# A cross-attention block and a feed-forward layer on one core: element-wise work spread over GpSimd and ScalarE, layer-one rows in strict turn, and a new order of all pieces

## The chip, the core and the metric

The kernel runs on one core of a Trainium2 chip. The core has a matrix engine (TensorE, PE in the profile; PEld is its weight load), three element-wise engines (VectorE or DVE, ScalarE or ACT, GpSimd or POOL), and queues that start transfers (SP, ACT and POOL issue them here). Each engine runs its own instructions in their order, and semaphores hold an instruction until what it needs is there. Matmuls write PSUM; the other tiles lie in SBUF. The metric is the time of one execution in microseconds (us).

## The reference

x is 8 batches x 8 heads x 512 rows x 64, state is 8 x 8 x 32 x 64. For each batch and head:

```python
scores = scale * np.matmul(x, state.transpose(0, 1, 3, 2))
scores = scores - scores.max(-1, keepdims=True)
a = np.exp(scores)
a /= a.sum(-1, keepdims=True) + 1e-09
xread = np.matmul(a, state)
```

The same is done the other way round (the state rows attend to x): sread. Both are laid side by side, 8 x 544 rows of 512, and go through two layers:

```python
h = x @ w_in              # 4352 x 512 by 512 x 2048
r = np.maximum(h, 0.0)
g = s * (r * r) + b
return (g @ w_out).astype(np.float32)
```

## The kernel before

**The algebra.** For the rows of x the kernel never forms xread: it multiplies the state with w_in first (M, 32 states x 4 heads on 128 partitions, two groups g) and then uses A, the transposed attention weights, as the moving operand, so that h = M^T A. Layer two sums g @ w_out in PSUM; s and b enter at the end (out = s * sum + bias). For batches 5, 6 and 7 and for the state rows layer two is a 2 x 2 block product with 7 instead of 8 products, for which sums of blocks of g (S) and of w_out (wsum, T1 to T4) are formed.

**Pieces and order.** All work is cut into pieces, and the constant ORDER (L15 to L75, nine strings) lists them. The loop at L713 takes them in that order, and each engine gets its instructions in that order; nothing is moved afterwards. An engine letter at the end (A ScalarE, V VectorE, G GpSimd) says who does a piece. For a batch b: x and xn load x in two layouts (GpSimd's queue; x waits, through a tiny GpSimd copy, for the transpose of the batch before, L180); xT transposes (VectorE); T are the score matmuls; U transposes the scores back (VectorE, from PSUM); mu takes the maxima and D subtracts them (L320); E1 is the exponential (ScalarE); z sums and inverts; At scales (L336) and A transposes (VectorE). keep copies the scores (ScalarE); nm, nms, E2, a2, aps, a2T, V, srd make sread. M.b.j.own are the matmuls of a quarter of M, own choosing one of two PSUM pairs, and Mc its copy to SBUF. l.b.f is one block of 128 layer-one rows for 512 tokens: two matmuls of 512 columns into one of two PSUM banks, then a relu on ScalarE (L449). lh is the same for half the tokens and two blocks (batch 0). s.b.f.n.e squares n blocks (L464), sh a half. L.b.rr.q is a quarter of a layer-two product for 128 tokens (4 matmuls), out its eviction and store. P, ev and put are products, evictions and stores of the 7-product form, 8 matmuls of 256 columns to a P; lsr, ssr, S_sr, P_sr, ev_sr are the same for the state rows. win and wout load the weights, turn and pair prepare the state, cps, c and bias make the bias, castx and casts convert what was loaded as float32, idle.n issues n matmuls whose result nobody reads.

**Tiles that bind pieces together.** Relu outputs lie in tiles of four blocks, three of them in a pool (L455, halves in four, L481). A tile comes free when all its squares are done. Two PSUM banks take layer-one results, two layer-two results, and two pairs of banks (own or not) everything else.

## Time and profile before

| | |
|---|---|
| median of 3 runs | 225.02 us (224.21 to 225.16) |
| the profiled execution | 224.36 us, of which the instructions span 222.2 us |
| TensorE busy | 210.7 us, 95% of the span |
| VectorE busy | 183.6 us, 83%, 267 instructions |
| ScalarE busy | 141.8 us, 64% |
| GpSimd busy | 43.4 us, 20%, mostly issue of transfers |
| granted TensorE clock | 1.0 |

Busy time says how long an engine had an instruction in work. An instruction that stands still after it started, because something it shares is taken, counts as busy. In the profile's rows `out<-in` names what is written and read, then the shape per operand, the number of instructions, the busy time and the mean duration in ns; what follows the second bar is the idle time of the engine before them and what ended it. In a timeline row the first number is the start in us from the span's start, the second the duration. Matmul rows overlap: one of 512 columns is shown 379 ns long while the next starts after 216.

### The profile page before, as it was taken

To read this page: it belongs to the slowest core of one execution; us is meant where nothing else is said; L and a number is where in the kernel's file an instruction comes from. 1 tells how busy PE (TensorE), PEld (TensorE's weight loads), DVE (VectorE), ACT (ScalarE), POOL (GpSimd) and SP (SyncE) were. 2 spreads that over 40 slices of the span, in tenths; PEclk is the share of its full clock that TensorE was granted. 3 is DMA by queue.
4 is the path that set the end of the run, shared out by engine and by line. 5 is a ranking of instruction groups with operands and counts; after the bars stand their busy time and mean duration, and the time that the engine had idled before them with its cause. 6 is when DMAs were issued, how large, how long until landed. Compare 5 with 4: busy or idle time off the path is not lost.

```text
span 222.2 us, 4473 instructions
## 1 busy us (share of the span) xinstructions
PE 210.7 (95%) x1816; PEld 115.8 (52%) x1816; DVE 183.6 (83%) x267; ACT 141.8 (64%) x243; POOL 43.4 (20%) x73
## 2 busy tenths in 40 slices
PE   6469999999999999999999999999999999999992
...
DVE  1597998889769997989796799889999997966772
...
POOL 8245504000273400046002160005200000000000
...
GB/s 158 227 207 206 205 193 58 101 72 20 100 112 117 112 174 50 16 100 120 192 47 133 96 128 124 49 45 101 141 2 65 127 0 3 94 99 0 3 134 149
DMA packets 23416, 22.67 MB, mean 102 GB/s; under 512 B 4196, under 2 KB 16996, under 8 KB 23396
## 3 DMA queue, kind: packets, MB, share of 16 engines
...
## 4 chain that ended last, share of the span: by engine, by line
PE 88%; DMA 4%; DVE 3%; ACT 3%; SPq 1%; issue 0%
PE ops L496 31%; PE hps L452 24%; PE opf_X L137 9%; PE opf_W L137 5%; PE mps L137 4%; DMA xf<-in_x_dram 4%; PE hps_sr L452 3%; PE opf_Y L137 2%; PE vps L137 2%; PE T_None L137 2%; PE aps L137 2%; PE ops_sr_X L137 2%; ACT M L152 1%; DVE xT L289 1%; PE ops_sr_W L137 1%; ACT rh L482 1%
## 5 line engine op out<-in xcount | busy, mean ns | idle before, releaser
L456 ACT ACTIVATE r<-hps 128x512 f16<-128x512 f32 x120 | 69.3, 610 | 29.8 <-PE hps L452 28.4
L496 PE MATMUL ops<-w_out,g 128*128 128x512 f16 x320 | 78.1, 379 | 1.3 <-DVE g L462 1.3
L452 PE MATMUL hps<-A,M 128*128 128x512 f16 x240 | 65.3, 380 | 0.5 <-DVE M L152 0.3
L496 PEld LDWEIGHTS <-g 128*128 128x128 f16 x320 | 30.3, 98 | 38.4 <-issue 2.8
L462 DVE TENSOR_TENSOR g<-r 128x1024 f16<-128x1024 f16 (+1 forms) x39 | 34.5, 897 | 8.1 <-ACT r L456 8.0
L452 PEld LDWEIGHTS <-M 128*128 128x128 f16 x240 | 21.9, 98 | 25.8 <-issue 4.7
L137 PEld LDWEIGHTS <-g 128*128 128x128 f16 x288 | 28.0, 98 | 6.4 <-issue 0.2
L152 ACT CAST M<-mps 128x1024 f16<-128x1024 f32 x28 | 28.0, 1013 | 1.8 <-PE mps L137 1.8
L192 POOL DMA_DIRECT2D xn<-in_x_dram x32 | 18.5, 588 | 29.2 <-PE vps L137 28.3
L506 DVE SCALAR_TENSOR_TENSOR osb<-ops,sb_bc,bias_bc 128x512 f32<-128x512 f32 x20 | 14.7, 734 | 1.0 <-PE ops L496 1.0
L180 POOL COPY ahead<-xT 1x2 f16<-1x2 f16 x5 | 1.8, 367 | 67.0 <-DVE xT L289 67.0
L456 ACT ACTIVATE r_sr<-hps_sr 128x256 f16<-128x256 f32 x16 | 6.2, 385 | 12.8 <-PE hps_sr L452 12.4
L564 DVE TENSOR_TENSOR g<-g 128x1024 f16<-128x1024 f16 x18 | 12.2, 685 | 2.0 <-PE opf_Y L137 1.9
L289 DVE STREAM_TRANSPOSE xT<-xh 128x1024 f32<-128x1024 f32 (+2 forms) x12 | 10.3, 871 | 3.2 <-ACT xh L152 3.2
L333 DVE TENSOR_REDUCE z<-E 128x32 f32<-128x1024 f16 (+1 forms) x9 | 9.9, 1095 | 3.7 <-ACT E L328 3.7
L137 PE MATMUL opf_X<-w_T,g 128*128 128x256 f16 x96 | 11.9, 273 | 0.0
L137 PE MATMUL mps<-w_in,stT 64*32 64x512 f16 x256 | 11.2, 383 | 0.2 <-ACT M L152 0.2
L318 DVE TENSOR_REDUCE mu<-U 128x32 f32<-128x1024 f32 (+1 forms) x9 | 9.9, 1097 | 0.2
L376 ACT ACTIVATE E<-T_None,nms 128x512 f16<-128x512 f32 x8 | 5.5, 691 | 6.9 <-DVE nms L372 4.4
L328 ACT ACTIVATE E<-Dm 128x1024 f16<-128x1024 f32 (+1 forms) x9 | 8.7, 963 | 1.8 <-DVE Dm L322 1.5
L322 DVE TENSOR_TENSOR Dm<-U,mu 128x1024 f32<-128x1024 f32 (+1 forms) x8 | 9.6, 1201 | 0.2
L314 DVE STREAM_TRANSPOSE U<-T_None 128x1024 f32<-128x1024 f32 x7 | 8.7, 1247 | 1.2 <-PE T_None L137 0.8
...
## 6 DMA issues: line engine op xcount, KB each, us to landing
...
w_in<-in_moe_w_in_dram POOLq DMA_DIRECT2D x8, 256.0 KB, 10.6
...
```

What stands on the lines that cost most here:

```text
L137: return nc.tensor.matmul(out, lhsT, rhs, start=start, stop=stop, tile_position=tp, is_transpose=is_transpose, skip_group_check=skip,)
L152: (engine.copy if engine is nc.scalar else engine.tensor_copy)(out, in_)
L192: nc.gpsimd.dma_start(out=xn_t[b][32 * jh : 32 * jh + 32].rearrange("t h c d -> t h (c d)"), in_=x[b].rearrange("h (t jh c) d -> jh t h (c ...
L289: nc.vector.transpose(part(out, p, g), part(in_, p, g))
L318: nc.vector.tensor_reduce(part(mu, p), blk(part(at[b]["U"], p)), AX.X, ALU.max)
L333: nc.vector.tensor_reduce(part(z, p), blk(part(at[b]["E1"], p)), AX.X, ALU.add)
L452: nc.tensor.matmul(hps, lhsT, rhs, start=(i == 0), stop=(i == len(terms) - 1))
L456: nc.scalar.activation(R_t[tag, q][:, i], hps, AF.Relu)
L462: e.tensor_mul(g, r, r)
L496: nc.tensor.matmul(ops_t[tag, rr], G_t[tag][:, f, P * rr : P * rr + P], w_out_f(f), start=(f == 0), stop=(f == NKF - 1),)
L506: nc.vector.scalar_tensor_tensor(osb, ops_t.pop((tag, rr)), s_bc, bias_bc, ALU.mult, ALU.add)
L564: e.tensor_tensor(out, x, y, op)
```

## The change

It edits three things. (1) ORDER is rewritten whole: the same pieces but for their engines, PSUM pairs and grouping. To GpSimd go the subtractions of maxima of batches 2, 4, 5 and 6 (that of batch 3 was there before), the At of batch 2, three more half squares of batch 0, ten squares of two blocks and one of four, block sums of batches 5 to 7 and of the state rows, and two weight sums. To ScalarE go squares of two blocks, seven of the eight squares of the state rows, and some evictions of M, while VectorE takes others and most a2T copies. In the first string the loads of x for batch 1 and of the later weights stand further back, partly behind squares on GpSimd. (2) The three relu tiles, and the four of half size, become single-buffer pools used in strict turn (`in_turn`). (3) The sums of blocks take a third choice, 2, for both halves in one instruction (`HALVES`).

```diff
-    "win.0 win.1 wout.0 x.1 win.2 wout.1 win.3 wout.2 wout.3 idle.11 castx.1.0.V castx.0.0.A xT.0.0.0 "
-    "casts.A turn.0.4.A pair.0.4 xT.0.1.0 T.0.1.0 U.0.0 mu.0.0 sb castx.1.1.A castx.0.1.A D.0.V.0 "
-    "xT.0.0.1 idle.6 xT.0.1.1 E1.0.0 T.0.0.1 keep.0.0 M.0.0.1 Mc.0.0.A z.0.0 At.0.V.0 A.0.0 idle.4 "
-    "M.0.1.1 Mc.0.1.A lh.0.0.0 U.0.1 mu.0.1 D.0.V.1 lh.0.2.0 keep.0.1 sh.0.0.0.V sh.0.2.0.V E1.0.1 z.0.1 "
-    "At.0.V.1 L.0.1.0 lh.0.6.0 sh.0.6.0.G L.0.0.0 M.1.0.1 Mc.1.0.A lh.0.4.0 A.0.1 lh.0.6.1 xT.1.0 "
-    "sh.0.4.0.G xT.1.1 T.1.1 U.1 lh.0.0.1 lh.0.4.1 lh.0.2.1 sh.0.2.1.G mu.1 M.0.2.0 Mc.0.2.A L.0.0.1 x.2 "
-    "L.0.1.1 st D.1.V sh.0.6.1.V keep.1 l.0.9 l.0.8 M.0.3.1 Mc.0.3.V l.0.10 s.0.8.2.V cps.0 cps.1 E1.1 "
-    "l.0.13 z.1 l.0.11 s.0.10.2.V At.1.V M.1.1.1 l.0.12 Mc.1.1.A l.0.14 l.0.15 L.0.0.2 s.0.12.2.A M.1.2.1 "
-    "A.1 s.0.14.2.V Mc.1.2.A cps.2 cps.3 c L.0.1.2 l.1.1",
...
+    "win.0 castx.0.0.V castx.1.0.A xT.0.1.0 casts.A xT.0.0.0 idle.12 pair.0.4 T.0.1.0 castx.1.1.A "
+    "turn.0.4.A M.0.0.0 U.0.0 mu.0.0 D.0.V.0 E1.0.0 idle.3 z.0.0 castx.0.1.V xT.0.0.1 keep.0.0 xT.0.1.1 "
+    "Mc.0.0.A T.0.0.1 keep.0.1 win.1 wout.0 M.0.1.1 At.0.V.0 A.0.0 Mc.0.1.A win.2 lh.0.2.0 x.1 U.0.1 "
+    "lh.0.0.0 sh.0.0.0.G sb mu.0.1 D.0.V.1 lh.0.6.0 idle.3 E1.0.1 z.0.1 At.0.V.1 A.0.1 lh.0.4.0 xT.1.0 "
+    "M.1.0.1 sh.0.2.0.G L.0.1.0 M.0.2.0 Mc.1.0.A M.1.2.1 Mc.1.2.V wout.1 L.0.0.0 Mc.0.2.A lh.0.6.1 "
+    "lh.0.4.1 cps.0 l.0.8 sh.0.4.0.G lh.0.2.1 xT.1.1 T.1.1 keep.1 sh.0.6.0.G l.0.10 l.0.9 L.0.0.1 "
+    "lh.0.0.1 U.1 mu.1 cps.1 l.0.11 win.3 sh.0.2.1.G M.0.3.1 Mc.0.3.A D.1.V E1.1 L.0.1.1 M.1.1.1 l.0.13 "
+    "l.0.15 wout.2 s.0.10.2.V s.0.8.2.V L.0.1.2 Mc.1.1.A l.0.14 z.1 l.0.12 s.0.12.2.A At.1.V A.1 L.0.0.2 "
+    "wout.3 s.0.14.2.A cps.2 cps.3 M.1.3.1 c",
+    "l.1.0 l.1.3 bias st pair.4.16 L.0.0.3 l.1.2 x.2 xT.2 Mc.1.3.A out.0.0 L.0.1.3 x.3 l.1.6 l.1.9 T.2.1 "
+    "keep.2 out.0.1 sh.0.0.1.V l.1.10 turn.4.12.A l.1.1 L.0.3.0 l.1.5 M.2.1.0 Mc.2.1.A sh.0.4.1.G "
+    "sh.0.6.1.G M.2.0.1 Mc.2.0.A U.2 mu.2 D.2.G L.0.2.0 L.0.3.1 s.1.0.4.V l.1.12 l.1.4 xT.3 T.3.1 E1.2 "
+    "M.2.2.0 l.1.14 x.4 l.1.13 L.0.3.2 l.1.7 l.1.11 U.3 L.0.2.1 z.2 At.2.G l.1.8 nm.3 nms.3.A E2.3.1 "
+    "E2.3.0 Mc.2.2.V A.2 s.1.4.4.V L.0.3.3 l.1.15 L.0.2.2 L.0.2.3 l.2.3 M.3.2.1 M.2.3.0 Mc.2.3.A l.2.6 "
+    "l.2.7 out.0.3 L.1.0.0 turn.12.16.A s.1.8.2.V s.1.10.2.V out.0.2 s.1.12.4.V l.2.2 l.2.10 mu.3 L.1.0.1 "
+    "Mc.3.2.A l.2.11 xn.3 L.1.1.0 a2.3 aps.3 xT.4 s.2.2.2.V l.2.1 L.1.1.1 l.2.5 x.5 a2T.3.V l.2.8 M.3.0.1 "
+    "Mc.3.0.A M.3.1.0 Mc.3.1.V",
...
+    "l.3.0 aps.4 out.1.2 l.3.8 l.3.11 T.5.1 a2T.4.V V.4 nm.5 nms.5.A E2.5.1 l.3.12 L.2.1.0 s.2.14.2.G U.5 "
+    "L.2.0.2 mu.5 l.3.5 E2.5.0 nm.2 z.4 s.2.12.2.G L.2.1.1 nms.2.A L.2.0.3 out.2.0 l.3.13 l.3.10 srd.4 "
+    "s.3.0.4.G L.2.1.2 l.3.6 At.4.V D.5.G l.3.15 L.2.1.3 out.2.1 M.5.1.1 l.3.9 s.3.8.2.V l.3.14 L.3.1.0 "
+    "l.3.7 L.2.2.0 s.3.6.2.A A.4 s.3.4.2.A L.2.2.1 M.4.3.1 M.5.0.0 L.2.2.2 Mc.5.0.A x.6 L.2.2.3 Mc.5.1.V "
...
+    "l.4.2 L.2.3.0 out.3.1 l.4.4 U.6 mu.6 D.6.G L.3.2.0 nm.6 l.4.6 L.2.3.1 L.2.3.2 A.5 L.2.3.3 out.2.3 "
+    "E1.6 z.6 L.3.2.1 s.4.0.2.G nms.6.A L.3.2.2 l.4.12 l.4.14 L.3.2.3 l.4.10 At.6.V l.4.15 L.3.0.0 "
+    "s.4.12.4.A L.3.0.1 E2.6.1 l.4.7 a2.2 E2.6.0 aps.2 out.3.2",
...
+    "l.5.13 l.5.8 a2.0 aps.0 a2T.0.A L.4.1.2 l.5.5 l.5.10 L.4.1.3 xn.0 l.5.14 wsum.T2.1.G l.5.6 L.4.0.2 "
+    "l.5.4 M.6.3.1 nm.7 Mc.6.3.A V.6.0 L.4.0.3 srd.0 srd.6 l.5.7 s.5.6.2.G U.7 wsum.T2.0.V s.5.4.2.A "
+    "M.7.2.0 out.4.1 xn.7 wsum.T4.0.V wsum.T4.1.V M.7.0.1 L.4.2.0 mu.7 A.6 l.6.11 l.6.9 nms.7.A L.4.2.1 "
+    "s.5.12.4.V s.5.8.4.V out.4.0 l.6.3 Mc.7.0.V P.5.0 l.6.15 l.6.1 E2.7.0 Mc.7.2.A L.4.2.2 L.4.2.3 nm.1 "
+    "D.7.V l.6.8 S.5.3.0.V S.5.1.0.V E1.7 P.5.1 l.6.13 E2.7.1 out.4.2 P.5.2 ev.5.X1 M.7.1.0 S.5.3.1.G "
+    "M.7.3.1 Mc.7.3.A l.6.12 S.5.2.0.V P.5.4 S.5.1.1.V S.5.2.1.V l.6.10 P.5.3 a2.7 ev.5.Y z.7",
+    "l.6.0 P.5.5 l.6.14 P.5.6 P.5.7 Mc.7.1.A l.6.6 aps.7 l.6.4 ev.5.X2 P.5.8 P.5.9 S.5.4.2.G ev.5.W1 "
+    "l.6.5 l.6.7 P.5.10 s.6.8.2.V s.6.10.2.V At.7.V A.7 s.6.12.4.V ev.5.X3 s.6.0.2.A nms.1.A l.6.2 "
+    "s.6.2.2.A a2T.7.V E2.1.0 P.5.11 E2.1.1 ev.5.W2 l.7.7 s.6.4.2.V s.6.6.2.V P.5.12 P.5.13 ev.5.X4 "
+    "S.6.3.0.V put.5.0.0 S.6.3.1.V l.7.3 P.6.0 P.6.1 l.7.1 S.6.1.2.V l.7.10 xn.1 V.7 srd.7 l.7.2 a2.1 "
+    "put.5.0.1 P.6.2 l.7.6 P.6.3",
+    "l.7.0 S.6.2.2.V ev.6.X1 P.6.4 l.7.8 aps.1 l.7.4 l.7.5 s.7.4.4.A ev.6.Y P.6.5 a2T.1.A ev.6.X2 l.7.15 "
+    "P.6.6 l.7.9 P.6.8 P.6.9 P.6.7 ev.6.W1 ev.6.X3 V.1 srd.1 l.7.13 S.6.4.2.G P.6.10 s.7.0.2.G s.7.2.2.G "
+    "l.7.12 lsr.3 P.6.11 l.7.14 put.5.1.0 put.5.1.1 l.7.11 S.7.3.0.V P.6.12 S.7.1.0.V ev.6.W2 put.6.0.0 "
+    "P.6.13 s.7.10.2.A lsr.11 s.7.8.2.V s.7.12.4.V P.7.0 lsr.2 lsr.7 ev.6.X4 P.7.1 S.7.3.1.V P.7.2 lsr.6 "
+    "lsr.5 ssr.2.2.A P.7.3 lsr.9 S.7.1.1.G S.7.2.2.V ev.7.X1 lsr.1 P.7.4",
+    "lsr.0 lsr.10 ssr.0.2.A P.7.6 lsr.8 ssr.8.2.A lsr.13 P.7.5 ssr.6.2.A ev.7.Y lsr.12 ssr.12.2.A ev.7.X2 "
+    "lsr.15 P.7.7 S.7.4.2.G ssr.10.2.A lsr.4 lsr.14 P.7.8 ssr.14.2.A P.7.9 ssr.4.2.V ev.7.W1 P_sr.0 "
+    "put.6.0.1 ev.7.X3 P.7.10 P.7.11 S_sr.3.0.G S_sr.1.2.G P.7.12 P.7.13 put.6.1.0 put.6.1.1 ev.7.W2 "
+    "ev_sr.0.0.X.0.0 P_sr.1 S_sr.2.2.V put.7.0.0 ev.7.X4 S_sr.4.0.G P_sr.2 ev_sr.0.1.X.0.0 put.7.0.1 "
+    "S_sr.3.1.G ev_sr.0.0.Y.1.1 put.7.1.0 put.7.1.1 S_sr.4.1.G P_sr.3 ev_sr.1.1.W.0.0 P_sr.4 P_sr.5 "
+    "ev_sr.1.1.X.1.1 ev_sr.0.1.W.1.1 P_sr.6 ev_sr.1.0.X.0.1",
@@ -446,13 +445,19 @@
             G_t[tag] = whole_t[tag][:, :, :ntok]
         return G_t[tag]
 
+    turns = {}
+
+    def in_turn(shape, name, tag, n):
+        k = turns[tag] = turns.get(tag, -1) + 1
+        return rpool.tile(shape, FP16, name=name, tag=f"{tag}{k % n}", bufs=1)
+
     def layer1(tag, f, terms, ntok):
         hps = ps_h.tile([P, ntok], FP32, name=f"hps_{tag}_{f}", tag="ph")
         for i, (lhsT, rhs) in enumerate(terms):
             nc.tensor.matmul(hps, lhsT, rhs, start=(i == 0), stop=(i == len(terms) - 1))
         q, i = f // 4, f % 4
         if (tag, q) not in R_t:
-            R_t[tag, q] = rpool.tile([P, 4, ntok], FP16, name=f"r_{tag}_{q}", tag="r")
+            R_t[tag, q] = in_turn([P, 4, ntok], f"r_{tag}_{q}", "r", 3)
         nc.scalar.activation(R_t[tag, q][:, i], hps, AF.Relu)
 
     def squared(e, g, r):
@@ -478,7 +483,7 @@
             for g in range(NG):
                 lhsT = M[:, g, P * (f + i) : P * (f + i) + P]
                 mm(hps[:, i, :], lhsT, part(A, p, g)[:, 0, :], start=(g == 0), stop=(g == NG - 1))
-        r = R_t[b, f, p] = rpool.tile([P, 2, HALF], FP16, name=f"rh_{b}_{f}_{p}", tag="rh", bufs=4)
+        r = R_t[b, f, p] = in_turn([P, 2, HALF], f"rh_{b}_{f}_{p}", "rh", 4)
         nc.scalar.activation(r, hps, AF.Relu)
 
     def square_half(b, f, p, e):
@@ -517,15 +522,16 @@
             store(b, rr, [rows.rearrange("(t r j) n -> r j t n", r=SCH, j=4)[rr]])
 
 
+    HALVES = (slice(0, 4), slice(4, 8), slice(0, 8))
     fast_w = {}
 
     def weight_sum(name, h, e):
 
         if name not in fast_w:
             fast_w[name] = konst.tile([P, NKF // 2, HALF], FP16, name=f"w_{name}", tag=f"w_{name}")
-        w = w_out16[:, 8 * h : 8 * h + 8]
-        B = [[w[:, k::2, HALF * n : HALF * n + HALF] for n in range(2)] for k in range(2)]
-        T = {k: t[:, 4 * h : 4 * h + 4] for k, t in fast_w.items()}
+        w = w_out16
+        B = [[w[:, k::2, HALF * n : HALF * n + HALF][:, HALVES[h]] for n in range(2)] for k in range(2)]
+        T = {k: t[:, HALVES[h]] for k, t in fast_w.items()}
         a, b = {
             "T1": lambda: (B[0][1], B[0][0]),
             "T2": lambda: (B[1][1], T["T1"]),
@@ -554,11 +560,12 @@
 
     def act_sum(b, name, h, e):
 
-        A = lambda i, j: block(b, i, j)[:, 4 * h : 4 * h + 4]
+        sl = HALVES[h]
+        A = lambda i, j: block(b, i, j)[:, sl]
         out, x, y, op = {
             1: lambda: (A(1, 0), A(1, 0), A(1, 1), ALU.add),
             2: lambda: (A(0, 0), A(1, 0), A(0, 0), ALU.subtract),
-            3: lambda: (fast(b, "S3")[:, 4 * h : 4 * h + 4], A(0, 0), A(1, 0), ALU.subtract),
+            3: lambda: (fast(b, "S3")[:, sl], A(0, 0), A(1, 0), ALU.subtract),
             4: lambda: (A(0, 1), A(0, 1), A(0, 0), ALU.subtract),
         }[name]()
         e.tensor_tensor(out, x, y, op)
@@ -618,7 +625,7 @@
             "S3": (A(0, 0), A(1, 0), ALU.subtract),
             "S4": (A(0, 1), S_sr("S2"), ALU.subtract),
         }[name]
-        out, x, y = (t[:, 4 * h : 4 * h + 4] for t in (S_sr(name), x, y))
+        out, x, y = (t[:, HALVES[h]] for t in (S_sr(name), x, y))
         e.tensor_tensor(out, x, y, op)
 
     def w_block(j, n):
```

## The prediction

> **What bounds the kernel now.** I read the page first (engine shares, slices, the chain that ended last), then the waits of TensorE, then the timeline of the start, then the pairs of VectorE and GpSimd instructions that ran at the same time, and last the groups by shape for prices.
>
> ```profile
> PE 210.7 (95%) x1816; PEld 115.8 (52%) x1816; DVE 183.6 (83%) x267; ACT 141.8 (64%) x243; POOL 43.4 (20%) x73
> ...
> PE   6469999999999999999999999999999999999992
> ...
> DVE  1597998889769997989796799889999997966772
> ...
> POOL 8245504000273400046002160005200000000000
> ...
> PE 88%; DMA 4%; DVE 3%; ACT 3%; SPq 1%; issue 0%
> ```
>
> TensorE is full from the fourth slice to the end. The second view, TensorE's waits between 31 and 218 us, has one entry:
>
> ```profile
> PE hps L452 <- ACT r L456: 0.2, 1, 0.2
> ```
>
> In the timeline matmuls of 512 columns start every 0.216 us there and those of 256 every 0.109, with 0.093 more at each change of tile shape; after 30.5 us no other gap is over 0.04 us. So only two things can shorten this kernel: the first 30 us, and the 4.1 us from the last matmul (218.1) to the end (222.2). Anything else can only lengthen it. The start:
>
> ```profile
> 10.36 0.62 ACT L152 CAST xh<-xf 128x512 f16<-128x512 f32 x1 [1.38 <-DMA xf<-in_x_dram]
> 10.89 0.62 ACT L328 ACTIVATE E<-Dm 128x512 f16<-128x512 f32 x1
> ...
> 12.66 1.01 ACT L152 CAST M<-mps 128x1024 f16<-128x1024 f32 x1 [0.68 <-PE mps L137]
> ...
> 13.40 0.71 DVE L358 STREAM_TRANSPOSE A<-At 128x512 f16<-128x512 f16 x1
> ...
> 16.07 0.75 DVE L462 TENSOR_TENSOR g<-rh 128x512 f16<-128x512 f16 x2
> ...
> 16.55 1.04 PE L496 MATMUL ops<-w_out,g 128*128 128x512 f16 x4 [1.35 <-DVE g L462]
> ```
>
> ScalarE's second cast of x waits for its transfer and holds the first exponential 1.3 us; the first A is ready at 14.1, layer one starts at 14.2, and the first layer two waits for squares. From 14.2 to 30.5 the matmul starts leave 3.4 us unused (1.5, 0.1, 0.2, 0.4, 0.4, 0.4, 0.4).
>
> The view for what the change adds, pairs of VectorE and GpSimd at one time:
>
> ```profile
> 24.16 1.04 POOL L462 TENSOR_TENSOR g<-rh 128x512 f16<-128x512 f16 x1 [2.24 <-ACT rh L482]
> 24.17 2.11 DVE L322 TENSOR_TENSOR Dm<-U,mu 128x1024 f32<-128x1024 f32 x1
> ...
> 37.12 1.06 POOL L462 TENSOR_TENSOR g<-rh 128x512 f16<-128x512 f16 x1
> 37.18 0.75 DVE L506 SCALAR_TENSOR_TENSOR osb<-ops,sb_bc,bias_bc 128x512 f32<-128x512 f32 x1
> ...
> 70.36 1.27 DVE L343 TENSOR_TENSOR At<-E,rz 128x1024 f16<-128x1024 f16 x1
> 70.50 1.14 POOL L180 COPY ahead<-xT 1x2 f16<-1x2 f16 x1 [4.02 <-DVE xT L289]
> ```
>
> A VectorE subtraction (median 1.22) took 2.11 beside a GpSimd square of 1.04: it stood still until that was over. A GpSimd copy of 0.17 took 1.14 behind a VectorE product. So two-operand work in SBUF on the two engines excludes each other. An eviction out of PSUM kept its 0.73 to 0.75, and a transpose beside the square at 18.74 its 0.71.
>
> **The change, part by part.** Prices:
>
> ```profile
> L462 DVE TENSOR_TENSOR g<-r 128x2048 f16<-128x2048 f16 x16 | 19.4, 1214 | 2.2 <-ACT r L456 2.1
> L460 ACT ACTIVATE g<-r 128x2048 f16<-128x2048 f16 x2 | 3.8, 1910 | 0.1
> L462 POOL TENSOR_TENSOR g<-rh 128x512 f16<-128x512 f16 x4 | 4.2, 1060 | 4.5 <-ACT rh L482 4.4
> L322 POOL TENSOR_TENSOR Dm<-U,mu 128x1024 f32<-128x1024 f32 x1 | 1.9, 1907 | 4.5 <-DVE mu L318 4.5
> ```
>
> Moved to GpSimd: 1024 f16 elements I take at 2 x 1.06 = 2.1 us and 2048 at 4.2 (lower ends 1.9 and 3.8, by the 1907 row). With 7 half squares (7.4 us), 5 subtractions (9.5), 10 squares of two (21), one of four (4.2), block sums of batches 5 to 7 (2 x 2.1 + 3 x 4.2 = 16.8), state-row sums (4 x 1.06 + 2.1 = 6.3), two weight sums (4.2) and one At (2.1), GpSimd computes 71.6 us instead of 6.1. The At has no row: 2.1 by size, or 4.0, since on VectorE its permuted write costs 1.29 against 0.68 for a square; I take 2.1; the other end is counted at l.2.6 below.
>
> All other engines, counted over both orders with these rows: VectorE 195.8 to 168.3 (the page's 183.6 is 0.94 of the sum, because neighbours overlap), ScalarE 157.7 to 166.3, TensorE the same 340 pieces with 73 changes of tile shape in each and 18 dummy matmuls for 21 (at the start, beside waits). So relief of VectorE is worth nothing by itself: TensorE did not wait for it after 31 us.
>
> The swaps of M evictions, a2T copies and nms between ScalarE and VectorE (1.01 against 1.21, 1.02 against 0.67, 0.20 against 0.17) and of M's PSUM banks lie beside matmuls: nothing. The last seven state-row products keep their order; before them GpSimd's chain (S_sr.3, S_sr.1, S_sr.4: 1.06 + 2.1, 0.7 on VectorE, 3 x 1.06 = 7.0 us) starts 8.7 us of matmuls ahead of its last reader, so the 4.1 us tail stays. The squares of batch 7 and S.6.4 on GpSimd (4.2 + 2 x 2.1) end 1.1 us before the relu of lsr.3, which takes their tile: nothing while the prices hold.
>
> The start, walked through the new order: win.0 still lands at 10.6. VectorE now casts x for g=0 (transfer at 5.2), so T begins at 6.9 (6.63 before). The exponential follows its subtraction at 9.9, not 10.9; but VectorE then does castx.0.1, two transposes (1.35 us) before At, and A.0.0 is ready at 14.4 (14.1 before). The first squares run on GpSimd: 16.5 to 18.6, so L.0.1.0 starts at 18.6 instead of 16.55, with four layer-one halves and M.1.0 ahead of it. x.1 is issued behind win.2 and lands at 20.4 instead of 17.8. wout.1, win.3, wout.2, wout.3 are queued behind GpSimd squares, that is behind relus: wout.3 is issued at 26 (16.8 before) and lands at 32.7, just ahead of cps.3. L.0.0.3 then waits 0.3 us for s.0.14 on ScalarE and ends at 36.15; before it ended at 36.03 with the bias product (0.22) still to come, so 36.25 for the same work: -0.1. (By unused TensorE time it is 2.7 us for 3.4, layer one 0.3 later: -0.4. I take the end, which holds everything.)
>
> After it, the exclusion and the strict turn together. The turn makes the relu that opens a new four-row tile wait for the squares of the tile three earlier. In the old order these squares always stand ahead of that relu; in the new one they stand behind it seven times (l.2.6, l.3.8, l.3.12, l.4.10, l.6.11, l.6.6, lsr.11), so the relu, and all of ScalarE behind it, waits for VectorE or GpSimd. I counted TensorE's slots along the order (0.216, 0.109, 0.093 for a change of shape, 10.9 us for the start) and looked at each place where a GpSimd operation meets a VectorE one or such a relu. Four are tight, times from the span's start:
> - T.3.1, due 44.4. D.2.G and s.1.0.4.V become ready within 0.5 us (41.1 to 41.7). If the square wins, xT.3 behind it ends at 44.2: 0. If the subtraction wins, the square waits 1.9 and T.3.1 starts at 46.1: 1.8. I take half, 0.9.
> - l.2.6, due 53.3: VectorE's A.2 waits for At.2.G (47.8 to 49.9), then s.1.4, out.0.3, s.1.8, s.1.10 end at 53.8: 0.2; with the At at 4.0 us 2.1, with the square first above 0. I take 0.2.
> - P.5.0, due 150.2, reads s.5.6.2.G, ready at 147.2 and 2.1 long. VectorE's s.5.12.4.V and s.5.8.4.V (1.21 each) come at 147.1 to 149.5. Between them GpSimd ends at 150.4 (0.2, but then s.5.8 holds relu l.6.3 and l.6.1: 0.8), behind both at 151.7 (1.5), ahead 0. I take 0.8.
> - l.6.5, due 166.1, needs the relu of l.6.6, which waits for s.6.10.2.V, which follows s.6.8.2.V behind S.5.4.2.G (4.2 us from 159.7 or, behind the scaling of a2.7, 160.5): the relu ends at 165.9 or 166.7: 0 to 1.0 with GpSimd a little late. I take 0.6.
>
> Waiting costs VectorE elsewhere too, but there it stays under TensorE: in the string from l.1.0 24.7 us of work plus 1.7 of expected waits (GpSimd's share times the expected rest of an operation, times nine instructions) against 27.4, from l.7.0 11.5 + 4.9 against 22.1.
>
> The last item hangs on whether the scaling of a2 (L385, one tensor operand) excludes GpSimd; no row shows the two together, so its ends are 0.1 and 0.6. [...]
>
> Sum: -0.1 + 0.9 + 0.2 + 0.8 + 0.6 = +2.4 us; ends -0.1 and +6.3. The profiled execution took 224.36 us (span 222.2) and would take 226.8; the median shown, 225.02, is 0.66 above it, so the forecast is 227.4.
>
> **The rivals.**
>
> Hidden anyway, 225.0: the four places come out at their lower ends and TensorE stays gapless. For it: from 155 to 172 us VectorE was busy 16.6 of 17.0 us and left no gap; its load now falls by 27 us. Against: 71.6 us of GpSimd work whose prices rest on five instructions.
>
> Faster, 223.4: the start closes half of the 3.4 us (1.6). For it: the exponential a microsecond earlier, M.0.0 at 10.8 instead of 12.2, three layer-one pieces of batch 0 ahead of L.0.0.1. Against: A.0.0, x.1 and the first L later. It decides if layer one starts by 14.2, unused time by 36 us is under 2 us and the waits after it are under 0.5.
>
> Slower through the clock, 227: dummy matmuls stand at 1.5 to 5.6 and 11.1 to 11.8, and between T (7.6) and M.0.0 (10.7) TensorE does almost nothing for 3.1 us; before, the longest hole was 2.3 us (9.0 to 11.5) and spacing stayed 0.216. The first six dummies started every 0.427. If that spacing comes back at 11 us, the 2.7 us of matmuls to 18.6 take double, of which 0.7 falls into waits: +2. [...] No row here shows a hole that long.
>
> The change not doing what it says: the strict turn may be the turn that tiles took before; the seven relus wait all the same, since three tiles are all there are.
>
> **How the numbers follow.** Exclusion and turn 0.42 (227.4), clock 0.08 (227), hidden 0.25 (225.0), start 0.25 (223.4). About 0.5%, 1.1 us, is what a measurement here tells from no change. Slower 0.50, within it 0.25, faster 0.25. The range goes down to the start's case and up to 230.0, where the two largest upper ends (1.8, 2.1) and the 0.8 and 0.6 meet (225.0 - 0.1 + 5.3 = 230.2); the slower case's own range is 226.2 to 230.0.
>
> **What would show it.** Gaps of TensorE at T.3.1, l.2.6, P.5.0 and l.6.5, and a VectorE square of 2 to 3 us beside D on GpSimd; ScalarE's relus of l.2.6 and l.6.6 released by VectorE squares; GpSimd rows of 2.1 and 4.2; first A at 14.4, first L at 18.6, x.1 at 20.4. Wrong if TensorE's waits after 36 us sum under 0.5 us; if GpSimd's rows are 1.3 times longer (then lsr.3's relu is 1.4 us late, and the time passes the range); or if x.1 or wout land 3 us later than walked.

## The result

| | before | after |
|---|---|---|
| median (lowest to highest, 4 runs each) | 225.09 us (224.21 to 225.94) | 231.12 us (230.32 to 231.65) |
| ratio, 95% interval | | 1.0265 (1.0215 to 1.0316) |
| the profiled execution, and its span | 224.36 us, 222.2 us | 230.93 us, 229.2 us |
| last matmul starts | 217.86 us | 223.65 us |
| from there to the end | 4.36 us | 5.51 us |

The changed kernel is slower by 6.0 us (its profiled execution by 6.6, between the spans 7.0). The forecast was 227.4 with a range up to 230.0, so the direction held and the size did not. The medians leave out an execution over 1.5% above the fastest of its kernel, such as the profiled one of e3 below (233.90 us at a granted clock of 0.968). From the page of the changed kernel, the engine shares, the slices of TensorE and of its clock, and the chain that ended last:

```profile
PE 214.3 (93%) x1813; PEld 116.6 (51%) x1813; DVE 172.1 (75%) x219; ACT 149.5 (65%) x257; POOL 108.4 (47%) x104
...
PE   7697989699999999999999999999799999999990
...
PEclk9859999999999999999999999999999999999999
...
PE 71%; DVE 13%; DMA 4%; ACT 4%; POOL 3%; issue 3%; DVEq 0%; ACTq 0%
```

GpSimd went from 20% to 47%, VectorE from 83% to 75%. But VectorE's share of the chain rose from 3% to 13%: it does less, and TensorE waits for it more. TensorE's row has a 6 in slice 8 (41 us) and a 7 in slice 29 (160 us), where it had nines from the fourth slice on, and PEclk drops to 5 in the third slice.

The waits of TensorE between 36 and 225 us (total, times, longest):

```profile
PE ops L501 <- DVE g L467: 1.9, 1, 1.9
PE opf_Y L136 <- DVE osb L511: 1.2, 1, 1.2
PE hps L457 <- DVE M L151: 0.4, 1, 0.4
```

Before, this view had one entry of 0.2. By start-to-start times, with the usual spacing and the 0.09 us of a change of tile shape taken off, the gaps of TensorE after 36 us sum to 4.5 us: 2.04 at L.0.3.0 (41.4 us), 1.36 at P.5.2 (160.3; the expectations below call this place P.5.3), 0.53 at a layer-one block that waits for the eviction Mc.5.3 (134.9), and 0.58 in six gaps of 0.04 to 0.29. The work that ended at 36.25 us before ends at 37.63, so 1.4 us was lost ahead of it. With the 1.15 us by which the tail grew, that makes the 7.0 us between the two spans. The two large gaps, the tail and the start follow.

**At 41 us.** The timeline of VectorE, GpSimd and TensorE, start and duration first:

```profile
38.63 1.25 DVE L288 STREAM_TRANSPOSE xT<-xh 128x1024 f32<-128x1024 f32 x1 [0.48 <-DMA xh<-in_x_dram]
...
39.80 1.36 DVE L511 SCALAR_TENSOR_TENSOR osb<-ops,sb_bc,bias_bc 128x512 f32<-128x512 f32 x2
...
39.94 0.17 POOL L179 COPY ahead<-xT 1x2 f16<-1x2 f16 x1 [9.74 <-DVE xT L288]
40.17 1.07 POOL L182 DMA_DIRECT2D xh<-in_x_dram  x2
...
41.08 2.51 DVE L467 TENSOR_TENSOR g<-rh 128x512 f16<-128x512 f16 x1
...
41.24 2.06 POOL L467 TENSOR_TENSOR g<-rh 128x512 f16<-128x512 f16 x2
...
43.65 0.61 PE L501 MATMUL ops<-w_out,g 128*128 128x512 f16 x2 [1.88 <-DVE g L467]
```

VectorE's half square sh.0.0.1 takes 2.51 us where that shape took 0.415 before. It starts 0.16 us ahead of two half squares that GpSimd does back to back, sh.0.4.1 and sh.0.6.1, while GpSimd is still issuing the load of x.3 (the row at 40.17), and it ends after both. L.0.3.0 reads its result.

**At 160 us.** The same view for the product P.5.2, whose bank out.4.2 has to empty:

```profile
154.38 2.32 POOL L191 DMA_DIRECT2D xn<-in_x_dram  x4
...
156.15 1.78 DVE L321 TENSOR_TENSOR Dm<-U,mu 128x1024 f32<-128x1024 f32 x1
156.72 3.19 POOL L571 TENSOR_TENSOR S<-g 128x1024 f16<-128x1024 f16 x1
157.85 2.60 DVE L571 TENSOR_TENSOR S<-g 128x1024 f16<-128x1024 f16 x1
160.49 0.69 DVE L571 TENSOR_TENSOR g<-g 128x1024 f16<-128x1024 f16 x1
161.10 0.74 DVE L511 SCALAR_TENSOR_TENSOR osb<-ops,sb_bc,bias_bc 128x512 f32<-128x512 f32 x1
```

D.7 (1.22 alone) starts while GpSimd is issuing four loads, and ends 1.22 us after the last of them. GpSimd's S.5.3.1, ready at 156.72, stands until D.7 is over, and S.5.3.0 on VectorE (the row at 157.85, 0.69 alone; the expectation of e3 calls it S.5.1.0) stands until S.5.3.1 is over. So the eviction out.4.2 (the last row) comes 1.2 us too late.

**The tail.** SyncE's queue and VectorE's last eviction:

```profile
221.37 0.55 SPq L706 DMA_DIRECT2D out_dram<-osr  x1
221.96 2.52 SPq L608 DMA_DIRECT2D out_dram<-osx  x4
...
223.96 0.48 DVE L702 SCALAR_TENSOR_TENSOR osr<-ops_sr_X,sb_bc,bias_bc 128x256 f32<-128x256 f32 x1 [0.39 <-PE ops_sr_X L136]
224.58 1.85 SPq L706 DMA_DIRECT2D out_dram<-osr  x3
```

Four stores of batch 7 (put.7) stand ahead of the last three stores of the state rows. Before, the four state-row stores were the last thing in the queue (217.00 to 219.51 us).

**The start.** Two places in the timeline of the first 33 us:

```profile
18.88 2.04 POOL L467 TENSOR_TENSOR g<-rh 128x512 f16<-128x512 f16 x2
19.02 2.47 DVE L344 TENSOR_TENSOR At<-E,rz 128x512 f16<-128x512 f16 x1
...
22.28 0.92 PE L136 MATMUL hph<-A,M 128*128 128x256 f16 x7 [1.27 <-DVE A L357]
...
25.53 1.04 POOL L467 TENSOR_TENSOR g<-rh 128x512 f16<-128x512 f16 x1 [3.38 <-ACT rh L487]
26.52 1.56 POOL L205 DMA_DIRECT2D w_out<-in_moe_w_out_dram  x2
28.06 1.04 POOL L225 DMA_DIRECT2D stn<-in_state_dram  x1
29.07 1.12 POOL L182 DMA_DIRECT2D xh<-in_x_dram  x2
...
32.12 1.02 PE L501 MATMUL ops<-w_out,g 128*128 128x512 f16 x4 [0.70 <-DMA w_out<-in_moe_w_out_dram]
```

At.0.V.1 takes 2.47 us (0.69 before) beside two more back-to-back squares. And GpSimd's queue holds the loads wout.2, wout.3, st and x.2 behind sh.0.2.1, which waited 3.4 us for its relu: x.2 is issued at 29.1 us and lands at 38.6 (before: 25.1 and 33.5).

Prices, from the groups by shape of the changed kernel, GpSimd first, then VectorE; the second number after the bar is the mean of one in ns:

```profile
L467 POOL TENSOR_TENSOR g<-r 128x1024 f16<-128x1024 f16 x10 | 19.0, 1917 | 20.4 <-ACT r L461 19.9 <-PE ops L501 0.5
L571 POOL TENSOR_TENSOR g<-g 128x2048 f16<-128x2048 f16 x3 | 12.2, 4064 | 20.4 <-PE opf_Y L136 20.4
```

```profile
L384 DVE TENSOR_SCALAR a<-E,q 128x512 f16<-128x512 f16 x16 | 10.9, 720 | 0.3
```

The scaling of a2 on VectorE, 350 ns each before, takes 720.

### The profile page after: what moved, and what is told of

It reads as the page before. It is cut to its first block, busy times and chain, and to the rows that moved or that the text cites. A ratio compares the mean times of both kernels' runs of the same rounds, so it can differ in the third digit from the quotient of the medians.

```text
span 229.2 us, 4475 instructions
## 1 busy us (share of the span) xinstructions
PE 214.3 (93%) x1813; PEld 116.6 (51%) x1813; DVE 172.1 (75%) x219; ACT 149.5 (65%) x257; POOL 108.4 (47%) x104
## 4 chain that ended last, share of the span: by engine, by line
PE 71%; DVE 13%; DMA 4%; ACT 4%; POOL 3%; issue 3%; DVEq 0%; ACTq 0%
PE ops L501 21%; PE hps L457 17%; PE opf_X L136 8%; PE opf_W L136 5%; DMA xh<-in_x_dram 4%; PE hps_sr L457 3%; PE mps L136 3%; PE opf_Y L136 2%; PE dps L667 2%; POOL g L467 2%; PE vps L136 2%; PE hph L136 2%; DVE g L467 2%; ACT r L461 2%; PE ops_sr_X L136 2%
## 5 line engine op out<-in xcount | busy, mean ns | idle before, releaser
L457 PE MATMUL hps<-A,M 128*128 128x512 f16 x240 | 66.5, 380 | 0.5 <-DVE M L151 0.4
L467 POOL TENSOR_TENSOR g<-r 128x1024 f16<-128x1024 f16 (+1 forms) x11 | 22.6, 2070 | 21.8 <-ACT r L461 21.2
L571 POOL TENSOR_TENSOR g<-g 128x2048 f16<-128x2048 f16 (+1 forms) x4 | 14.3, 3577 | 28.7 <-PE opf_Y L136 20.4
L151 ACT CAST M<-mps 128x1024 f16<-128x1024 f32 x23 | 22.9, 1012 | 1.5 <-PE mps L136 1.5
L467 DVE TENSOR_TENSOR g<-r 128x1024 f16<-128x1024 f16 (+1 forms) x23 | 20.4, 909 | 1.7 <-ACT r L461 1.7
L191 POOL DMA_DIRECT2D xn<-in_x_dram x32 | 18.6, 591 | 4.8 <-PE vps L136 3.8
L321 POOL TENSOR_TENSOR Dm<-U,mu 128x1024 f32<-128x1024 f32 x5 | 10.4, 2085 | 20.1 <-DVE mu L317 20.1
L465 ACT ACTIVATE g<-r 128x1024 f16<-128x1024 f16 (+1 forms) x13 | 15.1, 1185 | 0.2
L511 DVE SCALAR_TENSOR_TENSOR osb<-ops,sb_bc,bias_bc 128x512 f32<-128x512 f32 x20 | 14.4, 728 | 1.1 <-PE ops L501 1.1
L600 DVE SCALAR_TENSOR_TENSOR osx<-opf_X,sb_bc,bias_bc 128x512 f32<-128x512 f32 x9 | 6.6, 737 | 7.9 <-PE opf_X L136 7.7
L151 DVE CAST M<-mps 128x1024 f16<-128x1024 f32 x9 | 10.8, 1207 | 1.9 <-PE mps L136 1.9
L467 POOL TENSOR_TENSOR g<-rh 128x512 f16<-128x512 f16 x7 | 7.2, 1046 | 10.5 <-ACT sb_bc L640 7.1
```

The costliest lines, as they stand in the source:

```text
L151: (engine.copy if engine is nc.scalar else engine.tensor_copy)(out, in_)
L191: nc.gpsimd.dma_start(out=xn_t[b][32 * jh : 32 * jh + 32].rearrange("t h c d -> t h (c d)"), in_=x[b].rearrange("h (t jh c) d -> jh t h (c ...
L321: e.tensor_tensor(blk(part(Dm, p)), blk(part(at[b]["U"], p)), over_n(part(at[b]["mu"], p)), ALU.subtract)
L457: nc.tensor.matmul(hps, lhsT, rhs, start=(i == 0), stop=(i == len(terms) - 1))
L465: nc.scalar.activation(g, r, AF.Square)
L467: e.tensor_mul(g, r, r)
```

## The experiments

The theory after the result: VectorE and GpSimd shut each other out, and where the new order sets their operations side by side TensorE sees it; the tail is a matter of SyncE's queue. The rivals: the new order or the strict turn costs the time whoever does the work; the loads in GpSimd's queue are late; the lower clock at the start.

| run | edit to the changed kernel | median us | ratio to before, 95% |
|---|---|---|---|
| e1 | 29 operations back to VectorE | 248.47 | 1.1024 (1.0942 to 1.1106) |
| e2 | two half squares to VectorE | 231.50 | 1.0293 (1.0201 to 1.0385) |
| e3 | S.5.3.1 to VectorE | 229.34 | 1.0202 (1.0137 to 1.0267) |
| e4 | last stores issued by ScalarE | 230.17 | 1.0251 (1.0176 to 1.0325) |
| e5 | four loads ahead of one square | 230.04 | 1.0235 (1.0179 to 1.0291) |
| e6 | e3 + e4 + e5 | 227.68 | 1.0142 (1.0093 to 1.0191) |
| e7 | no strict turn | 231.71 | 1.0310 (1.0244 to 1.0376) |
| e8 | kernel before, four D on GpSimd | 224.67 | 1.0004 (0.9974 to 1.0034) |
| e9 | e6 + e2 + win.3 ahead of a square | 226.68 | 1.0088 (1.0057 to 1.0119) |
| e10 | e9 + six dummy matmuls | 226.91 | 1.0111 (1.0063 to 1.0158) |
| e11 | e9 + xT.2 behind c | 226.51 | 1.0067 (1.0044 to 1.0090) |
| e12 | e11 + s.3.0.4 to VectorE, Mc.5.3 earlier | 233.28 | 1.0362 (1.0328 to 1.0395) |
| e13 | all loads ahead of all squares | 229.16 | 1.0183 (1.0130 to 1.0236) |
| e14 | e13 + the mends, s.3.0.4 left on GpSimd | 225.00 | 1.0017 (0.9989 to 1.0045) |

### e1: the work back on VectorE

```diff
- ... sh.0.0.0.G ... D.2.G ... At.2.G ... s.3.0.4.G ... S.5.3.1.G ... S_sr.4.1.G ...
+ ... sh.0.0.0.V ... D.2.V ... At.2.V ... s.3.0.4.V ... S.5.3.1.V ... S_sr.4.1.V ...
```

> The changed kernel, but 29 of the 31 operations that the change newly gave to GpSimd are done by VectorE at the same place of the order (two squares, s.2.12.2 and s.5.6.2, stay on GpSimd). Order, strict turn and tail are unchanged. Theory (VectorE and GpSimd shut each other out): VectorE's scaling of a2 falls back from 720 ns to about 350, the gap of 2.0 us at L.0.3.0 and that of 1.4 us at P.5.3 shrink to under 0.3 each, and the time is about 228 us; the later start (1.1) and the longer tail (1.2) stay. Rival (the new order and the strict turn cost the time, whoever does the work): the two gaps stay and the time is 230 to 232 us. Second rival (GpSimd really relieved VectorE): VectorE is late now and the time is over 232 us.

It took 248.47 us, 17 more than the changed kernel, so the second rival came closest, in a way nobody had: VectorE was busy 182 us (74% of the span), so it is not full, but it does its work in order, and the places in the order were written for GpSimd. The first and a later gap of TensorE, 4.3 and 4.6 us, are such places. At 18.4 us L.0.1.0 needs sh.0.2.0, which now stands on VectorE behind a reduction that waits for an exponential, behind At, A and xT.1.0. The timeline of e1:

```profile
19.12 0.69 DVE L332 TENSOR_REDUCE z<-E 128x16 f32<-128x512 f16 x1 [0.70 <-ACT E L327]
...
21.91 0.67 DVE L288 STREAM_TRANSPOSE xT<-xh 128x512 f32<-128x512 f32 x1
...
22.50 0.38 DVE L467 TENSOR_TENSOR g<-rh 128x512 f16<-128x512 f16 x1
22.94 1.03 PE L501 MATMUL ops<-w_out,g 128*128 128x512 f16 x2 [4.18 <-DVE g L467]
```

Of the two gaps that the run was made for, the one at P.5.2 was gone, and at L.0.3.0 1.06 us was left, where the theory had under 0.3 for each. The part of the theory on the scaling is clean here. The scaling of a2 in the groups of e1, with GpSimd nearly out of the way:

```profile
L384 DVE TENSOR_SCALAR a<-E,q 128x512 f16<-128x512 f16 x16 | 5.1, 361 | 0.3
```

720 ns beside GpSimd's work, 361 without, 350 before: an instruction with one tensor operand is held too. The mutual hold is real, and giving the work back is no cure, because this order was written for two queues.

### e2: the two half squares at 41 us

```diff
- ... sh.0.4.1.G sh.0.6.1.G M.2.0.1 ...
+ ... sh.0.4.1.V sh.0.6.1.V M.2.0.1 ...
```

> The changed kernel, but the two half squares sh.0.4.1 and sh.0.6.1 go from GpSimd to VectorE. Theory: sh.0.0.1 on VectorE stood 2.1 us behind them; it takes 0.41 us now, the gap at L.0.3.0 falls from 2.0 to about 0.1 us, the squares cost VectorE 0.8 us that TensorE does not see, and the time is about 229.2 us. Rival (the load of x for batch 2 is late, the transpose with it and all that VectorE has behind it): the gap stays above 1 us and the time within 0.5 us of 231.

Measured 231.50, no gain. The three half squares took 1.09 us on VectorE and the gap at L.0.3.0 was gone, as the theory said. In its place came 1.0 us at T.2.1 and 1.6 us at T.3.1, where VectorE's transposes waited for x. From the timeline of e2:

```profile
48.46 1.25 DVE L288 STREAM_TRANSPOSE xT<-xh 128x1024 f32<-128x1024 f32 x1 [0.93 <-DMA xh<-in_x_dram]
```

x.3 landed at 48.3. It is issued only when xT.2 is done, and xT.2 waited for x.2. So there are two causes at this place, and the gap that is seen is the larger of them. Not all of it is the edit's: this execution was already 0.9 us behind the changed kernel's at 33 us, ahead of the edit, and x.2 landed at 40.4 and not at 38.6. The wait at T.3.1 comes back in e9 (1.56). At T.2.1 and T.3.1 the gaps given for the experiments hold the 0.09 us of the change of shape.

### e3: the block sum at 160 us

```diff
- ... M.7.1.0 S.5.3.1.G M.7.3.1 ...
+ ... M.7.1.0 S.5.3.1.V M.7.3.1 ...
```

> The changed kernel, but the block sum S.5.3.1 goes from GpSimd to VectorE. Theory: D.7 and S.5.1.0 on VectorE no longer wait beside it (1.8 and 2.6 us fall to 1.2 and 0.7), the eviction out.4.2 comes in time and the gap of 1.36 us ahead of P.5.3 goes: about 229.8 us. Rival (VectorE is simply full there, since it held 16.6 of 17 us before): the 0.7 us more on VectorE keep the gap at 0.7 us or more and the time above 230.5.

229.34 us, 1.8 under the changed kernel (229.10 to 229.90, against 230.32 to 231.65); the gap of 1.36 was gone. The timeline of this place is shown from e6 below, which holds this edit:

```profile
155.39 1.22 DVE L321 TENSOR_TENSOR Dm<-U,mu 128x1024 f32<-128x1024 f32 x1
156.52 0.68 DVE L571 TENSOR_TENSOR S<-g 128x1024 f16<-128x1024 f16 x1
...
158.24 0.75 DVE L511 SCALAR_TENSOR_TENSOR osb<-ops,sb_bc,bias_bc 128x512 f32<-128x512 f32 x1 [0.31 <-PE ops L501]
```

The subtraction is back at 1.22 and the block sum at 0.68, and now VectorE waits for TensorE. VectorE had room for the work; it had no room to be held.

### e4: the queue of the last stores

```diff
-            nc.sync.dma_start(out_sr[i][:, :, sl], out[:, sl])
+            nc.scalar.dma_start(out_sr[i][:, :, sl], out[:, sl])
```

> The changed kernel, but the last four stores of the state rows are issued by ScalarE, not behind the stores of batch 7 in SyncE's queue. Theory (the tail grew because the last stores stand behind four stores of batch 7 in that queue): the time from the last matmul's start to the end falls from 5.45 to about 4.2 us, and the time is about 229.9 us. Rival (the transfers themselves are slower, because more of them run at the end): the tail stays above 5 us and the time at 231.

In the profile the tail fell from 5.51 to 4.07 us, which is 0.3 us shorter than in the kernel before. The median is 230.17, 0.95 under the changed kernel's, with intervals that overlap; the tail itself is the measure. The queues of SyncE and ScalarE in the timeline of e4:

```profile
217.54 5.22 SPq L608 DMA_DIRECT2D out_dram<-osx  x8
...
221.16 3.65 ACTq L706 DMA_DIRECT2D out_dram<-osr  x4
```

The last store is issued at 224.26 us, right behind its eviction (223.75); before the edit that was 225.87 for 223.96.

### e5: four loads ahead of a square

```diff
- ... win.3 sh.0.2.1.G ... wout.2 s.0.10.2.V ... wout.3 s.0.14.2.A ... bias st pair.4.16 ... x.2 xT.2 ...
+ ... win.3 wout.2 wout.3 st x.2 sh.0.2.1.G ... s.0.10.2.V ... s.0.14.2.A ... bias pair.4.16 ... xT.2 ...
```

> The changed kernel, but in GpSimd's queue the loads wout.2, wout.3, st and x.2 stand ahead of the half square sh.0.2.1 (behind win.3) instead of behind it; every computation is where it was, those on GpSimd too. Theory (the square, which waits for a relu until 25.5 us, holds the loads behind it in GpSimd's queue; x.2 is issued at 29.1 us instead of about 25 and lands at 38.6, so the transpose xT.2, the evictions and sh.0.0.1 on VectorE and the two half squares on GpSimd, which stand behind the load of x.3, all come late and meet): x.2 is issued by 25.5 us, the wait for wout.2 (0.9 with the change of shape) and the gap of 2.0 us at L.0.3.0 are gone, together 2.5 to 3 us, and the time is about 228.4 us. Rival (the exclusion alone makes the gap): the gap at L.0.3.0 stays above 1.5 us and the time above 230.

x.2 was issued at 24.81 instead of 29.07, as expected, and the gap with the wait for wout.2 fell from 0.87 to 0.20. But x.2 landed only 0.9 us earlier (37.73), 12.9 us after its issue where the changed kernel had 9.5; win.3, wout.2, wout.3 and st were issued in the 3.8 us ahead of it, which is probably the reason; no run was made for that. The gap at L.0.3.0 stayed at 1.75, and the median was 230.04. The rival on the exclusion was right about that gap. The timeline of e5 says why it cannot be moved by a load:

```profile
37.76 1.25 DVE L288 STREAM_TRANSPOSE xT<-xh 128x1024 f32<-128x1024 f32 x1
38.93 1.37 DVE L511 SCALAR_TENSOR_TENSOR osb<-ops,sb_bc,bias_bc 128x512 f32<-128x512 f32 x2
39.07 0.17 POOL L179 COPY ahead<-xT 1x2 f16<-1x2 f16 x1 [12.05 <-DVE xT L288]
39.30 1.14 POOL L182 DMA_DIRECT2D xh<-in_x_dram  x2
40.21 2.58 DVE L467 TENSOR_TENSOR g<-rh 128x512 f16<-128x512 f16 x1
40.44 2.06 POOL L467 TENSOR_TENSOR g<-rh 128x512 f16<-128x512 f16 x2
```

Both queues hang on xT.2. VectorE does two evictions after it and comes to sh.0.0.1 2.45 us after xT.2 began; GpSimd waits for xT.2, issues x.3 and comes to its squares 2.68 us after xT.2 began. In the changed kernel these were 2.45 and 2.61, in the run with all loads in front 2.41 and 2.66. The order itself makes them meet, whenever x.2 lands.

### e6: three mends at once

The edits of e3, e4 and e5 together.

> The loads moved as in the run with the loads first, S.5.3.1 on VectorE, and the last four stores issued by ScalarE. If the three causes stand beside each other: 231.1 - 2.7 - 1.4 - 1.3 = 225.7 us. If one mend only moves the wait to the next place (as the two half squares on VectorE did): 227.5 us or more.

227.68 us: above the 225.7 of "beside each other" and within the rival's bound. The tail (4.07) and P.5.2 (no gap) came in full; 1.55 us stayed at L.0.3.0 and 2.16 us ahead of the layer-one half that waits for A.0.1.

### e7: without the strict turn

```diff
-            R_t[tag, q] = in_turn([P, 4, ntok], f"r_{tag}_{q}", "r", 3)
+            R_t[tag, q] = rpool.tile([P, 4, ntok], FP16, name=f"r_{tag}_{q}", tag="r")
```

The half tiles likewise.

> The changed kernel with the relu tiles in pools of three and four buffers as before, not in strict turn. Theory (the turn binds nothing here: the relus that wait would wait for one of three tiles all the same): 231 us, within 1 us, and the same gaps. Rival (the turn holds relus that a free tile could have taken): the gaps of 0.1 to 0.5 us after 47 us go and the time falls by 1 us or more.

231.71 us against 231.12, intervals overlapping, and the same gaps: 1.95 at L.0.3.0, 1.37 at P.5.2, 0.53 and 0.29 where they were. The turn makes no difference that can be measured here.

### e8: four subtractions on GpSimd in the old order

```diff
- ... D.2.V ... D.4.V ... D.5.V ... D.6.V ...
+ ... D.2.G ... D.4.G ... D.5.G ... D.6.G ...
```

> The kernel before with only the subtractions D.2, D.4, D.5 and D.6 on GpSimd. Theory (exclusion costs only where VectorE has no slack): VectorE's rows beside them grow by up to 1.9 us each, each subtraction takes 1.9 to 2.8 us instead of 1.2, layer one of a batch comes up to 1.6 us later than before, and TensorE waits 0 to 2 us in all: 225 to 227 us. Rival (a dependent chain through GpSimd is always seen by TensorE): four gaps of about 0.7 to 1.5 us, 228 us or more.

No difference that can be measured (ratio 1.0004, 0.9974 to 1.0034). The holds are there. In the groups by shape of e8, first GpSimd's subtraction, then VectorE's four-block squares (1214 before) and its scaling (350 before):

```profile
L322 POOL TENSOR_TENSOR Dm<-U,mu 128x1024 f32<-128x1024 f32 x5 | 10.7, 2140 | 44.7 <-DVE mu L318 25.7 <-ACT r L456 19.0
```

```profile
L462 DVE TENSOR_TENSOR g<-r 128x2048 f16<-128x2048 f16 x16 | 21.0, 1315 | 2.6 <-ACT r L456 2.5
...
L385 DVE TENSOR_SCALAR a<-E,q 128x512 f16<-128x512 f16 x16 | 5.9, 410 | 0.4
```

TensorE saw one new gap of 0.5 us at 135.9 us. In this order the exclusion cost nothing that can be measured in the time, though three exponentials on ScalarE waited 3.7 us in all, the longest 2.8, for subtractions on GpSimd.

### e9 and e10: both causes at 41 us, and the clock

```diff
- ... l.0.8 sh.0.4.0.G ... win.3 ... sh.0.4.1.G sh.0.6.1.G ...
+ ... l.0.8 win.3 sh.0.4.0.G ... sh.0.4.1.V sh.0.6.1.V ...
```

> The three mends together (loads first, S.5.3.1 on VectorE, last four stores on ScalarE's queue), and two more: the half squares sh.0.4.1 and sh.0.6.1 go to VectorE, and the load win.3 stands ahead of the half square sh.0.4.0 in GpSimd's queue, so that the squares sh.0.4.0 and sh.0.6.0 begin 1.3 us later. Theory (a gap has two causes that stand beside each other, the late load and the two squares back to back; only both mends together close it): no gap over 0.3 us at T.2.1, L.0.3.0 and T.3.1, that is 1.5 us less than the run with three mends. At.0.V.1 ends ahead of the squares now (about 0.7 us long, not 2.5 to 3.2), A.0.1 comes 1.3 us earlier and the wait of 2 us for it falls under 1: together about 225.0 us. Rival (each mend moves the wait on): 227 us or more. If only one of the two new mends does what it says: 226.1 to 226.5.

226.68 us, between the theory's 225.0 and the rival's 227. The gaps at T.2.1 and L.0.3.0 were gone, and the gap ahead of the half that needs A.0.1 fell from 2.16 to 0.28, because GpSimd issued win.3 (19.96 to 21.2 us) when At.0.V.1 ran, which took 1.56 us and not 3.16. What stayed is 1.56 us at T.3.1: x.3, issued at 39.25, landed at 45.8. So "each mend moves the wait on" was right once more, at one place.

e10 adds six dummy matmuls to e9:

```diff
- "turn.0.4.A M.0.0.0 U.0.0 ...
+ "turn.0.4.A idle.6 M.0.0.0 U.0.0 ...
```

> The five mends and six dummy matmuls more, ahead of M.0.0.0, in the hole of 1.9 to 2.5 us. Theory (the start is set by the chain through VectorE, GpSimd and the loads, not by TensorE's clock): layer one runs every 0.109 us instead of 0.213 from its start, but the matmul that follows the wait for A.0.1 starts within 0.4 us of where it does without the dummies, and the time is the same within 0.6 us. Rival (the lower clock at the start lengthens it): about 1.5 us less than with the five mends alone.

226.91, the same. But the dummies did not do what they were for: layer one's halves still started every 0.213 us from 14.5 to 15.9 us, where the kernel before has 0.109 at a granted clock of 1.0. So this run says nothing on the clock.

### e11 and e12: xT.2 earlier, and one square too many

```diff
- ... M.1.3.1 c", "l.1.0 ... l.1.2 xT.2 Mc.1.3.A ...
+ ... M.1.3.1 c xT.2", "l.1.0 ... l.1.2 Mc.1.3.A ...
```

> The five mends, and VectorE does the transpose xT.2 directly behind the bias scaling c, ahead of the copy of the bias. Theory (the last gap, 1.6 us at T.3.1, comes from the load of x.3, which is issued only once xT.2 is done; xT.2 stood behind the bias copy and the state transposes): xT.2 starts at about 35.8 instead of 37.7 us, x.3 is issued at about 37.4 instead of 39.3 and lands 1.9 us earlier, the gap at T.3.1 falls under 0.2, and the time is about 225.2 us. Rival (the subtraction on GpSimd and the four-block square meet there again and hold xT.3): the gap stays above 1 us and the time at 226.7.

226.51. x.2 landed at 37.23 and xT.2 waited 1.9 us for it, so it ran at 37.25, not 35.8; x.3 was issued 0.5 us earlier than in e9 and landed 2.0 us earlier. The gap at T.3.1 fell from 1.56 to 0.60, but 0.69 came back at T.2.1, which waits for the state transposes that now stand behind xT.2, and 1.08 us stood at the wait for wout.1, which landed at 25.89. The theory's link was right (x.3 waits for xT.2), and its start time was wrong: the load decides.

```diff
- ... s.3.0.4.G ... s.5.0.2.V L.4.3.1 L.4.3.2 L.4.3.3 Mc.5.3.V E2.0.0 ...
+ ... s.3.0.4.V ... L.4.3.1 L.4.3.2 L.4.3.3 Mc.5.3.V s.5.0.2.V E2.0.0 ...
```

> The six mends, and two more: the square s.3.0.4 goes from GpSimd to VectorE, and VectorE does the eviction Mc.5.3 ahead of the square s.5.0.2. Theory: the gaps of 0.35 us at 92.7 (behind that square) and of 0.5 us at 133.8 (layer one waiting for that eviction) go, and the time is about 0.8 us under the run with six mends, 224.4 us, no different from the kernel before. Rival (the square is not what holds U.5, or it delays VectorE as much): the gap at 92.7 stays, 224.9 us or more.

233.28 us, 6.8 more than e11, a case neither side had. The eviction Mc.5.3 did its part: the gap of 0.53 at 133 us was gone. The square did not. From the timeline of e12:

```profile
94.20 1.22 DVE L467 TENSOR_TENSOR g<-r 128x2048 f16<-128x2048 f16 x1
...
95.51 1.09 ACT L461 ACTIVATE r<-hps 128x512 f16<-128x512 f32 x2 [7.04 <-DVE g L467]
```

On GpSimd it ran from about 85 us (e9), the moment its relus were there. On VectorE it stands behind U.5, three reductions and an eviction until 94.2, and the relu that takes its tile waits 7 us for it. TensorE stood 5.1 us, and its matmuls then started every 0.427 us until 99 us. It is one of the 29 operations of e1, whose later gap of 4.6 us lies at the same layer-two product.

### e13 and e14: all loads in front

```diff
- ... x.1 U.0.1 lh.0.0.0 sh.0.0.0.G sb mu.0.1 D.0.V.1 ... sh.0.2.0.G L.0.1.0 ... wout.1 ... win.3 ... wout.2 ... wout.3 ... st ... x.2 ...
+ ... x.1 U.0.1 lh.0.0.0 sb wout.1 win.3 wout.2 wout.3 st x.2 mu.0.1 D.0.V.1 sh.0.2.0.V sh.0.0.0.V ... L.0.1.0 ...
```

> The changed kernel, but wout.1, win.3, wout.2, wout.3, st and x.2 are issued right behind x.1, ahead of every square on GpSimd, and the first two half squares (sh.0.2.0, sh.0.0.0) are VectorE's, behind D.0.V.1. Theory (the loads held behind squares in GpSimd's queue make the late start and, through x.2 and x.3, the waits at L.0.3.0): x.2 lands by 34.5 us instead of 38.6, the wait for wout.2 (0.9) goes, the bias matmul starts at 35.5 or earlier (36.6), and the time is 228.0 to 229.5 us. Rival (the transfers are limited by what the queues carry, not by when they are issued): x.2 lands after 36.5 us again and the time is above 230.3.

229.16 us, 2.0 under the changed kernel. x.2 landed at 34.92 (the theory's bound was 34.5, the rival's 36.5), the wait for wout.2 fell from 0.87 to 0.24, and the bias matmul started at 35.02 instead of 36.56 (36.04 in the kernel before). At L.0.3.0 1.56 us stayed, as in e5. The run also moved the first two half squares to VectorE; what each of the two edits gave was not separated.

e14 adds the other mends: e2, e3, e4, xT.2 behind c, and Mc.5.3 ahead of s.5.0.2.

> All loads in front as in the run before it, with S.5.3.1 and the two half squares sh.0.4.1 and sh.0.6.1 on VectorE, the last stores on ScalarE's queue, xT.2 behind c, and Mc.5.3 ahead of s.5.0.2; s.3.0.4 stays on GpSimd. If the rest of 1.5 us was the loads: no gap over 0.3 us at T.2.1, L.0.3.0 and T.3.1, none at 133 us, 224.0 us, no slower than the kernel before. Rival (the rest is the clock at the start and the spread of the small gaps): 225.5 us or more.

225.00 us, against 224.87 for the kernel before in the same comparison: no difference that can be measured, and 6.1 us under the changed kernel. The waits of TensorE in e14 from 36 us to the end:

```profile
PE T_None L136 <- DVE xT L288: 0.3, 1, 0.3
```

T.3.1 keeps a gap of 0.44, 0.09 of it the change of shape. In the profiled execution the last matmul starts 0.85 us later than before, the tail is 0.30 shorter, and the gaps after 36 us sum to 0.9; the work of the first 36 us is done at 36.24, level with before (36.25). The theory's 224.0 was missed by 1.0, the rival's 225.5 by 0.5. None of the runs beats the kernel before.

## Why the prediction was right and wrong

**What bounds.** That only the first 30 us and the tail could gain, and all else could only lengthen, held. No gain came from either.

**Prices.** GpSimd's operations cost what was taken: 1.05 for a half square, 1.92 for two blocks (2.1 forecast), 3.6 for four blocks and 4.06 for a long block sum (4.2), 1.91 for the At (2.1). Its computing sums to 71.0 us (71.6). First A at 13.4 (14.4), first L at 18.3 (18.6), x.1 at 20.0 (20.4).

**Exclusion.** Right, and what was left undecided is settled: the scaling of a2 is held too (720 ns in the mean, 361 with GpSimd's work taken away in e1). But no run shows the 0.6 that the sum took for l.6.5: S.5.4.2 on GpSimd started at 166.43 us, after the scaling of a2.7 (164.54, 0.62 for its two instructions), so the two did not meet, and the place gave no gap.

**The four places.** The mechanism was right and the places were wrong. T.3.1 was put at 0.9 and gave 0.05: the square of VectorE started first (45.92 us), and D.2.G on GpSimd (46.15) took 2.76 instead. l.2.6 (0.2), P.5.0 (0.8) and l.6.5 (0.6) gave nothing. The 2.5 us forecast for the four came out at 0.05. Instead the holds cost 2.04 at L.0.3.0 and 1.36 at P.5.2. The step that failed is the look "at each place where a GpSimd operation meets a VectorE one". At L.0.3.0 the two meet because both queues hang on xT.2, through the tiny copy ahead of x.3; that wait of GpSimd's was not walked. At P.5.2 the held operations are not read by TensorE; it waits for an eviction two places behind them on VectorE. I looked for late readers of the held results and not for who is queued behind them.

**The start, -0.1.** It was +1.4. The walk followed x.1 and the weights to 36 us and let At.0.V.1 pass at 0.69; it took 2.47 beside two squares. wout.3's issue was put at 26 and its landing at 32.7; it was issued at 27.3 and landed at 34.9, and TensorE waited 0.7 us for wout.2 (landed 32.07). x.2 behind them was not walked at all. e13 shows the size, its two moved squares included: with the loads ahead of the squares the kernel gains 2.0 us. A part of the 1.4 is probably the clock's, as told under the rivals.

**"The 4.1 us tail stays."** It grew by 1.15. The step followed GpSimd's chain of sums, which was in time, and passed over SyncE's queue, where put.7 had moved ahead of three of the last four stores. e4 shows it: another queue for them, and 1.44 us are gone.

**The rivals.** The strict turn may be the turn tiles took before: right, by e7. That relieving VectorE is worth nothing by itself held too; but e1 and e12 show the other side, that in the new order its operations cannot go back. The clock did fall: the dummies start every 0.427 us until 6.1, layer one's halves every 0.213 from 13.5 to 16.6, and the granted clock is 0.5 from 10.1 to 17.0 us, 0.984 in the mean. The hole of 3.1 us that the prediction asked about was cut in two, waits of 1.73 and 0.51 us between 7.3 and 10.0, and the rate fell all the same. The clock does not account for the 6 us: e14 has a clock of 0.983 and the same half rate there, and takes the time of the kernel before. But it is not free. The kernel before ran beside each experiment too; its 27 executions with a mean clock of 0.997 or more took 224.26 us in the median, its 32 with 0.985 to 0.992 took 225.1. And of four profiles with nearly the same order up to 36 us, e4 with 3.4 us of half rate (mean granted clock 0.990) lost 1.1 us by then, the changed kernel with 6.8 (0.984) lost 1.4, e2 with 6.8 (0.981) lost 2.3 and e7 with 10.2 (0.977) lost 3.3. So a part of the start's 1.4 us is probably the clock's; how much was not separated, since the dummies of e10 did not raise it.

**The sum.** Forecast +2.4, measured +6.0. Missing are L.0.3.0 (2.0), P.5.2 (1.4), the tail (1.15), the start (1.5 more than forecast), the eviction Mc.5.3 (0.5) and small gaps (0.5); too much were the four places (2.4). These parts come from the profiled executions, whose spans differ by 7.0, or 4.6 over the forecast; the medians differ by 6.0. The range ended at 230.0 since it was built of the four places' upper ends alone, and had nothing for queues that were costed at nothing.
